# Rows of v 160 bytes apart in SBUF instead of 130, and two q and two k buffers fewer: an attention-and-FFN kernel on one core

## The chip, the cores and the metric

The kernel runs on one core of one Trainium2 chip. The metric is the device time of one execution in microseconds (us). Runs of the two kernels of a comparison alternate on one chip.

In the views, PE is the TensorE, PEld its weight loads, DVE the VectorE, ACT the ScalarE, POOL the GpSimd and SP the SyncE. A run of bytes is a stretch of adjacent bytes that one packet writes. A load has landed when its last completion event has come. k2 is the load of k for block 2, and so on.

## The reference, cut to what matters

```python
# q, k, v: (4, 8, 768, 64) f32; 4 sink positions, window 128
scores = scale * np.matmul(q, k.transpose(0, 1, 3, 2))
keep = is_sink | in_window          # a query sees 4 sinks and the last 128 keys
a = softmax(np.where(keep, scores, -1e9))
x = np.matmul(a, v)                 # -> (3072, 512)
xn = x / rms(x) * rms_g
out = (silu(xn @ w_gate) * (xn @ w_val)) @ w_out    # d_ff 1536
```

The work is cut into 24 blocks of 128 query positions (4 batches of 6). Each block needs its own q, k and v: three loads of 128 rows x 8 heads x 64 numbers.

## The kernel before: the parts that matter

```python
VW = D + 1                          # 65: 64 numbers of v and a 1.0 that sums the weights
LD = 16                             # buffers for q, and as many for k
ld  = ctx.enter_context(tc.tile_pool(name="ld", bufs=LD))
vld = ctx.enter_context(tc.tile_pool(name="vld", bufs=B))
...
V16 = {b: vld.tile([P, NT, H, VW], BF16, name="v16") for b in range(B)}
...
for b in range(B):                  # the column of ones
    dve(60, lambda b=b: nc.vector.memset(V16[b][:, :, :, D:VW], 1.0), ...)
...
def load_v(g):                      # f32 in HBM, cast to bf16 by the load
    b, t = divmod(g, NT)
    nc.gpsimd.dma_start(out=V16[b][:, t, :, 0:D], in_=block_of(v, g))
...
def av(g, u):                       # the matmuls that read v
    ...
    nc.tensor.matmul(
        out=dest, lhsT=T["e", g, u][:, x, 0, :], rhs=V16[b][:, t, h, :],
        start=(t == 0), stop=True, skip_group_check=True,
    )
```

A row of `V16` is one head of one position: 64 bf16 of v, 128 bytes, and then the 1.0. With `VW = 65` rows lie 130 bytes apart, so few start on a multiple of 32. The program decides the order of all instructions at build time with a small model of the engines (`Plan`); `LD` is also a constraint of that model: a load of q or k of block g comes after the transpose of block g - LD.

The softmax here doesn't subtract the row's maximum and nothing guards it: scores larger than these inputs give would overflow.

Of the kernel before, what the change touches and what calls it, by code (L numbers as in the profile page):

```python
# [12 lines left out]
BF16 = mybir.dt.bfloat16  # L13
I32 = mybir.dt.int32

P = 128
# [10 lines left out]
class Plan:  # L27
# [9 lines left out]
    def __init__(self):  # L37
        self.ops, self.held = [], {}
        self.rings = {"POOL": 0, "HW": 0, "TR": 0}
        self.banks = {i: 0 for i in range(8)}  # L40
# [8 lines left out]
    def land(self, ring, first, work):  # L49
# [3 lines left out]
        if ring == "POOL":  # L53
            begin = max(first, r["POOL"], r["HW"])
            r["POOL"] = begin + (1.4 * work if begin < 8500 else work)
            self.loads -= 1
            return r["POOL"] + 520
        if ring == "HW":
            begin = max(first, r["HW"])
            r["HW"] = begin + (1.25 * work if begin > 2500 else work)  # L60
            return r["HW"] + 900
        begin = max(first, r["TR"], r["POOL"])
# [74 lines left out]
def kernel(  # L137
# [15 lines left out]
    B, H, S, D = q.shape  # L153
# [5 lines left out]
    NT = S // P  # L159
# [5 lines left out]
    NG = NB // GB  # L165
    GN = GB * P
    VW = D + 1
    HW = 4 * VW
    SW = P // HP
    inv_sqrt_d = 1.0 / math.sqrt(D)  # L170
# [9 lines left out]
    POOL_MASK_FROM = 16  # L180
    X_DMA_FROM = 9
    QK_DMA_FROM = 8
    LD = 16
    GATE_FROM = 6
    LOAD_LEAD = 9
    LEAD_FROM = 10
# [7 lines left out]
    const = ctx.enter_context(tc.tile_pool(name="const", bufs=1))  # L194
    ld = ctx.enter_context(tc.tile_pool(name="ld", bufs=LD))
    vld = ctx.enter_context(tc.tile_pool(name="vld", bufs=B))
# [16 lines left out]
    def bank(slot):  # L213
        name = "_".join(str(x) for y in slot for x in (y if isinstance(y, tuple) else (y,)))
        BANK[slot] = ring.tile([P, 512], FP32, name=name, tag=f"bank{plan.held[slot]}")
        return BANK[slot]
# [10 lines left out]
    sel = const.tile([P, P], BF16, name="sel")  # L227
    headm = const.tile([P, H], FP32, name="headm")
    grow = const.tile([1, DM], FP32, name="grow")
    V16 = {b: vld.tile([P, NT, H, VW], BF16, name="v16") for b in range(B)}  # L230
    T = {}


# [18 lines left out]
    for b in range(B):  # L252
        dve(60, lambda b=b: nc.vector.memset(V16[b][:, :, :, D:VW], 1.0),
            gives=[("vone", b)], prio=-97 + b if b == 0 else -50)
# [54 lines left out]
    def block_of(src, g):  # L309
        b, t = divmod(g, NT)  # L310
        return src[b, :, t * P:(t + 1) * P, :].rearrange("h t d -> t h d")
# [9 lines left out]
    def load_bf16(name, src, g):  # L321
        T[name, g] = ld.tile([P, H, D], BF16, name=name)
        nc.gpsimd.dma_start(out=T[name, g], in_=block_of(src, g))  # L323

    def load_v(g):
        b, t = divmod(g, NT)
        nc.gpsimd.dma_start(out=V16[b][:, t, :, 0:D], in_=block_of(v, g))  # L327

# [4 lines left out]
    for i, name in enumerate(F32_LOADS):  # L333
        n, g, e = name[0], int(name[2:]), {"s": "SP", "a": "ACT"}[name[1]]
# [7 lines left out]
        out=grow, in_=moe_rms_g.rearrange("(o d) -> o d", o=1)))}, (), ["grow"], -89.5,  # L342
# [5 lines left out]
    def sw_load(fn, gives, work, ns=870, needs=()):  # L348
        n = len(issue)
        more = [("sw", n - DEPTH)] if n >= DEPTH else []  # L350
        op({"POOL": (ns, 1900, fn)}, list(needs) + more, list(gives) + [("sw", n)], -89 + n,
           ring="POOL", work=work)
        issue.append(n)

    def sw_block(g, what="qkv"):
        for n in what:
# [3 lines left out]
            else:  # L360
                src = q if n == "q" else k
                needs += [(n + "T", g - LD)] if g >= LD else []
                sw_load(lambda n=n, src=src, g=g: load_bf16(n, src, g), [(n, g)], 860,
# [137 lines left out]
    def av(g, u):  # L501
        b, t = divmod(g, NT)
        pv = bank(("av", g, u))
        if t >= 2:
            nc.tensor.matmul(  # L505
                out=pv[:, 0:HW], lhsT=T["esk", g], rhs=T["vsk", b][:, 4 * u:4 * u + 4, :],
                start=True, stop=False, skip_group_check=True,
            )
        for j in range(2):
            for hi in range(2):  # L510
                h = 4 * u + 2 * j + hi
                x = 2 * hi + j
                dest = pv[:, (h - 4 * u) * VW:(h - 4 * u + 1) * VW]
                if t >= 1:
                    nc.tensor.matmul(  # L515
                        out=dest, lhsT=T["e", g - 1, u][:, x, 1, :],
                        rhs=V16[b][:, t - 1, h, :],
                        start=(t == 1), stop=False, skip_group_check=True,
                    )
                nc.tensor.matmul(  # L520
                    out=dest, lhsT=T["e", g, u][:, x, 0, :], rhs=V16[b][:, t, h, :],
                    start=(t == 0), stop=True, skip_group_check=True,
                )
        T.pop(("e", g - 1, u), None)

    def normal(g, u):
        if u == 0:
            T["x16", g] = xpool.tile([P, H, D], BF16, name="x16")
        pvv = BANK.pop(("av", g, u))[:, 0:HW].rearrange("p (h c) -> p h c", c=VW)
        rden = small.tile([P, 4], FP32, name="rden")  # L530
# [72 lines left out]
    def sink_v(b, half):  # L603
        nc.tensor.matmul(
            out=bank(("vs", b, half))[:, 0:HW], lhsT=sel,
            rhs=V16[b][:, 0, 4 * half:4 * half + 4, :], start=True, stop=True,
        )

    def sink_vm(b, half):
        if half == 0:  # L610
            T["vsk", b] = sink.tile([P, H, VW], BF16, name="vsk")
        hs = slice(half * 4, half * 4 + 4)
# [34 lines left out]
    for g in range(NB):  # L647
        b, t = divmod(g, NT)
# [40 lines left out]
        for u in range(2):  # L689
            xs = [[("x", g, u, hi, n) for hi in range(2)] for n in range(nq)]  # L690
            if g < PE_MASKS:
                es = xs
            elif g < POOL_MASK_FROM or t == 0:
                dve(600 if nq == 2 else 335, lambda g=g, u=u: mask_dve(g, u),
                    sum(xs, []) + ["masks"], [("e", g, u)], early)
                es = [[("e", g, u)]] * nq
            else:
                es = []
                for n in range(nq):
                    pool(590, lambda g=g, u=u, n=n: mask_pool(g, u, n), sum(xs, []),  # L700
                         [("e", g, u, n)], g)
                    es.append([("e", g, u, n)])
            T["es", g, u] = es
            needs = es[0] + (T["es", g - 1, u][1] if t else []) + [("v", g), ("vone", b)]
            needs += [("v", g - 1)] if t else []
            needs += [("esk", b, t), ("vsk", b, 0), ("vsk", b, 1)] if t >= 2 else []
            needs += [("av", g - 1, u)] if g else []
            pe((130, 242, 354)[min(t, 2)], lambda g=g, u=u: av(g, u), needs, [("av", g, u)],
               pa + 5, takes=[("av", g, u)])
            dve(548, lambda g=g, u=u: normal(g, u),  # L710
                [("av", g, u)] + ([("xr", g - 3)] if g >= 3 else [])
                + ([("n", g - 1, u)] if g else []), [("n", g, u)], early, drops=[("av", g, u)])
# [19 lines left out]
        if t == 0:  # L732
            dve(600, lambda b=b: sink_k(b),
                [("kT", g), ("s", g + 1)] + ([("ss", b - 2, i) for i in ((2, 4) if b - 2 < 2 else (2,))]
                               if b >= 2 else []), [("ksk", b)], 0.1 * g)
            for half in range(2):
                pe(115, lambda b=b, half=half: sink_v(b, half), [("v", g), ("vone", b), "sel", ("s", g)],
                   [("vs", b, half)], pa + 14, takes=[("vs", b, half)])
                dve(340, lambda b=b, half=half: sink_vm(b, half), [("vs", b, half), "headm"]
                    + ([("av", NT * (b - 2) + NT - 1, u) for u in range(2)] if b >= 2 else [])  # L740
                    + ([("vsk", b, 0)] if half else []),
                    [("vsk", b, half)], 0.1 * g, drops=[("vs", b, half)])
            for t0, n in ((2, 2), (4, 2)) if b < 2 else ((2, 4),):
                pe(n * 53 + 16, lambda b=b, t0=t0, n=n: sink_s(b, t0, n),
                   [("ksk", b), ("s", g + 1)] + [("qT", g + t0 + i) for i in range(n)],
                   [("ss", b, t0)], -1000.0 + 10 * (g + t0) + 2, takes=[("ss", b, t0)], mode=3)
                act(n * 107 + 55, lambda b=b, t0=t0, n=n: sink_e(b, t0, n),
                    [("ss", b, t0), "table"] + ([("av", g - 1, u) for u in range(2)] if b else []),
                    [("esk", b, t0 + i) for i in range(n)], early, drops=[("ss", b, t0)])
# [169 lines left out]
```

## Time and profile before

| | |
|---|---|
| time, median of the first 3 runs | 246.64 us (246.4 to 246.71) |
| span of the profiled execution | 244.3 us |
| TensorE (PE) busy | 232.6 us, 95% |
| transfers queued by GpSimd (POOL), share of 16 engines | 81.0% (76.6% in another execution of the same kernel, e2 below) |
| q, k and v loads | 70, 128 KB each in SBUF, median 10.4 to 10.9 us from issue to landing |
| matmuls that read v | 352 of 65 columns, 8 of 260 |

The page of the profile gives busy times, then forty slices of the span, the transfer queues and the chain of work that ended last. A busy engine need not be one that sets the time; the chain and the waits say which one does. The lines themselves stand in the prediction.

### The profile page before, as it was taken

What the parts mean: (1) busy time and instruction counts of PE and PEld (TensorE: products, weight loads), DVE (VectorE), ACT (ScalarE), POOL (GpSimd) and SP (SyncE); (2) the same over time, 40 slices, a digit from 0 to 9 for tenths busy, and PEclk for the clock granted to TensorE, in tenths of its full rate; (3) what the DMA queues carried; (4) which work ended last, traced back from release to release, by engine and by line L of the source; (5) the groups of instructions that cost most, each with busy time, mean ns of one, the idle gap of its engine ahead of it and who ended that gap; (6) DMA issues with size and microseconds to landing.
All of it is one profiled execution on the core that took longest, in us unless ns stands there. A gap on an engine that the chain in (4) does not pass through costs nothing.

```text
span 244.3 us, 5510 instructions
## 1 busy us (share of the span) xinstructions
PE 232.6 (95%) x2098; PEld 147.8 (61%) x2120; DVE 183.7 (75%) x482; ACT 131.2 (54%) x276; POOL 88.8 (36%) x114
## 2 busy tenths in 40 slices
PE   4978999999999999999999999999999999999994
PEld 2557996875789765688875444444545544444443
DVE  4388979979899998899888499991299992377700
ACT  3886466778675837654537555735745521333111
POOL 8995755695444749423004200302504200000000
PEclk9999999999999999999999999999999999999999
DMA  8999999999999999999944544014311013200022
GB/s 112 172 170 195 192 188 188 156 146 174 171 196 130 156 124 179 142 216 133 149 35 107 133 107 86 3 21 108 120 34 21 4 21 107 86 3 0 0 86 86
DMA packets 111979, 27.22 MB, mean 111 GB/s; under 512 B 102097, under 2 KB 109009, under 8 KB 111954
## 3 DMA queue, kind: packets, MB, share of 16 engines
q0 software_dynamic: 80704, 13.90, 81.0%
q1 hardware_dynamic: 31106, 12.85, 27.0%
q8 instruction: 16, 0.26, 0.5%
q10 hardware_dynamic: 144, 0.13, 0.2%
q14 instruction: 9, 0.07, 0.1%
HBM read 28.31 MB, written 6.29 MB: 142 GB/s over the span
## 4 chain that ended last, share of the span: by engine, by line
PE 77%; DVE 9%; POOL 5%; DMA 4%; issue 3%; ACT 0%; POOLq 0%; DVEq 0%; ACTq 0%
PE o L790 23%; PE g L757 21%; PE v L757 21%; PE s L456 4%; DMA wg<-in_moe_w_gate_dram 4%; DVE hT L780 2%; PE av L520 2%; DVE p L770 2%; PE av L515 2%; DVE r L560 2%; POOL v L327 1%; DVE xr L564 1%; PE av L505 1%; PE o_last L808 1%; DVE x L532 1%
## 5 line engine op out<-in xcount | busy, mean ns | idle before, releaser
L757 PE MATMUL g<-xnt,wg 128*128 128x128 bf16 (+2 forms) x525 | 69.8, 282 | 1.6 <-DMA wg<-in_moe_w_gate_dram 1.2
L757 PE MATMUL v<-xnt,wv 128*128 128x128 bf16 (+2 forms) x522 | 71.0, 281 | 0.3
L764 ACT ACTIVATE th<-g 128x512 bf16<-128x512 f32 x72 | 42.9, 600 | 46.7 <-PE g L757 45.2
L790 PE MATMUL o<-wo,hT 128*128 128x512 bf16 x263 | 62.6, 379 | 1.2 <-issue 0.6
L770 DVE SCALAR_TENSOR_TENSOR p<-th,g 128x512 bf16<-128x512 bf16 x72 | 48.1, 683 | 16.6 <-ACT th L764 16.2
L757 PEld LDWEIGHTS <-wg 128*128 128x128 bf16 x528 | 43.1, 98 | 21.0 <-DMA wg<-in_moe_w_gate_dram 1.5
L757 PEld LDWEIGHTS <-wv 128*128 128x128 bf16 x528 | 42.6, 98 | 18.5 <-issue 0.8
L469 ACT ACTIVATE e<-s 128x512 bf16<-128x512 f32 (+1 forms) x104 | 48.4, 542 | 6.6 <-PE s L456 6.3
L780 DVE TENSOR_TENSOR hT<-p,v 128x512 bf16<-128x512 bf16 x72 | 47.2, 682 | 1.5 <-PE v L757 0.6
L790 PEld LDWEIGHTS <-hT 128*128 128x128 bf16 x276 | 25.6, 98 | 28.7 <-issue 1.3
L491 POOL TENSOR_SCALAR_AFFINE_SELECT e<-e 128x512 bf16<-128x512 bf16 x14 | 9.4, 680 | 61.8 <-ACT e L469 48.8
L798 ACT ACTIVATE osb<-o 128x512 f32<-128x512 f32 x23 | 13.8, 599 | 29.0 <-PE o L790 29.0
L323 POOL DMA_DIRECT2D k<-in_k_dram x23 | 20.5, 890 | 15.9 <-DMA v<-in_v_dram 7.0
L323 POOL DMA_DIRECT2D q<-in_q_dram x23 | 20.5, 893 | 13.0 <-DMA k<-in_k_dram 3.8
L327 POOL DMA_DIRECT2D v<-in_v_dram x24 | 21.3, 889 | 10.0 <-DMA q<-in_q_dram 6.0
L532 DVE TENSOR_TENSOR x<-av,rden 128x256 bf16<-128x256 f32 x48 | 20.4, 425 | 1.7
L540 ACT ACTIVATE sq<-x 128x512 bf16<-128x512 bf16 x24 | 15.2, 632 | 9.4 <-DVE x L532 9.3
L531 DVE RECIPROCAL rden<-av 128x4 f32<-128x4 f32 x48 | 8.5, 177 | 15.4 <-PE av L520 15.3
L486 DVE TENSOR_TENSOR e<-e,masks 128x1024 bf16<-128x1024 bf16 (+1 forms) x30 | 18.9, 650 | 1.0 <-ACT e L469 0.8
L564 DVE SCALAR_TENSOR_TENSOR xr<-x,r,gb 128x512 bf16<-128x512 bf16 x24 | 19.0, 790 | 0.9
L520 PE MATMUL av<-v,e 128*128 128x65 bf16 x192 | 16.9, 194 | 0.0
L515 PE MATMUL av<-v,e 128*128 128x65 bf16 x160 | 15.0, 193 | 0.0
(70 smaller groups left out, 177.2 us busy)
## 6 DMA issues: line engine op xcount, KB each, us to landing
out_dram<-osb SPq DMA_DIRECT2D x23, 256.0 KB, 2.2
v<-in_v_dram POOLq DMA_DIRECT2D x24, 128.0 KB, 10.4
q<-in_q_dram POOLq DMA_DIRECT2D x23, 128.0 KB, 10.9
k<-in_k_dram POOLq DMA_DIRECT2D x23, 128.0 KB, 10.8
wo<-in_moe_w_out_dram POOLq DMA_DIRECT2D x2, 768.0 KB, 12.0
wg<-in_moe_w_gate_dram POOLq DMA_DIRECT2D x4, 256.0 KB, 7.8
wv<-in_moe_w_val_dram POOLq DMA_DIRECT2D x4, 256.0 KB, 8.2
wg<-in_moe_w_gate_dram POOLq DMA_DIRECT2D x1, 384.0 KB, 9.4
```

Source lines behind the costliest of these rows:

```text
L323: nc.gpsimd.dma_start(out=T[name, g], in_=block_of(src, g))
L327: nc.gpsimd.dma_start(out=V16[b][:, t, :, 0:D], in_=block_of(v, g))
L469: nc.scalar.activation(out=T["e", g, u][:, 2 * hi:2 * hi + 2, n0:n1, :].rearrange("p x n c -> p x (n c)"), in_=ps.rearrange("p (j c) -> p ...
L515: nc.tensor.matmul(out=dest, lhsT=T["e", g - 1, u][:, x, 1, :], rhs=V16[b][:, t - 1, h, :], start=(t == 1), stop=False, skip_group_check=True,
L520: nc.tensor.matmul(out=dest, lhsT=T["e", g, u][:, x, 0, :], rhs=V16[b][:, t, h, :], start=(t == 0), stop=True, skip_group_check=True,)
L532: nc.vector.tensor_tensor(out=T["x16", g][:, 4 * u:4 * u + 4, :], in0=pvv[:, :, 0:D], in1=rden.unsqueeze(2).to_broadcast((P, 4, D)), op=AL ...
L564: nc.vector.scalar_tensor_tensor(out=T["xr", g], in0=T.pop(("x16", g)).rearrange("p h d -> p (h d)"), scalar=r[:, 3:4], in1=gb, op0=ALU.mu ...
L757: nc.tensor.matmul(out=ps[:, i * n:(i + 1) * n], lhsT=w_sb[:, kt, ft * P:(ft + 1) * P], rhs=T["xnt", G][:, kt, cols], start=(kt == 0), sto ...
L764: nc.scalar.activation(out=T["th", key], in_=BANK[("g", key)], func=ACT.Tanh, scale=0.5,)
L770: nc.vector.scalar_tensor_tensor(out=T["p1", key], in0=T.pop(("th", key)), scalar=1.0, in1=BANK.pop(("g", key)), op0=ALU.add, op1=ALU.mult,)
L780: nc.vector.tensor_tensor(out=T[hk][:, i:i + n, cols], in0=T.pop(("p1", key)).rearrange("p (n c) -> p n c", n=n), in1=BANK.pop(("v", key)) ...
L790: nc.tensor.matmul(out=BANK[("o", G, tb)], lhsT=T["h", G, ft // 4][:, ft % 4, tb * P:(tb + 1) * P], rhs=wo[:, ft, :], start=(ft == 0), sto ...
```

## The change

The intent: every 128-byte run of v that a load writes is to start on a multiple of 32 bytes and fill whole 32-byte pieces, so that no neighbouring bytes have to be kept. That any are kept otherwise was a guess. The price is memory: 4 batches x 48 rows x 30 bytes = 5,760 bytes on each partition. With all 16 q/k buffers that does not fit: the builder then finds 8.625 KB left for the last pool, which needs 10. Two q and two k buffers fewer free 4 KB.

```diff
+    VS = 80
...
-    LD = 16
+    LD = 14
...
-    V16 = {b: vld.tile([P, NT, H, VW], BF16, name="v16") for b in range(B)}
+    V16 = {b: vld.tile([P, NT, H, VS], BF16, name="v16") for b in range(B)}
...
-                        rhs=V16[b][:, t - 1, h, :],
+                        rhs=V16[b][:, t - 1, h, 0:VW],
...
-                    out=dest, lhsT=T["e", g, u][:, x, 0, :], rhs=V16[b][:, t, h, :],
+                    out=dest, lhsT=T["e", g, u][:, x, 0, :], rhs=V16[b][:, t, h, 0:VW],
...
-            rhs=V16[b][:, 0, 4 * half:4 * half + 4, :], start=True, stop=True,
+            rhs=V16[b][:, 0, 4 * half:4 * half + 4, 0:VW], start=True, stop=True,
```

## The prediction

> **What bounds the kernel now.** I read the page from the top: busy shares, the forty slices, the chain that ended last. The first question for a change of layout is whether transfers, the TensorE or something else sets the end.
>
> ```profile
> PE 232.6 (95%) x2098; PEld 147.8 (61%) x2120; DVE 183.7 (75%) x482; ACT 131.2 (54%) x276; POOL 88.8 (36%) x114
> PE   4978999999999999999999999999999999999994
> DMA  8999999999999999999944544014311013200022
> PE 77%; DVE 9%; POOL 5%; DMA 4%; issue 3%; ACT 0%; POOLq 0%; DVEq 0%; ACTq 0%
> ```
>
> The TensorE (PE) is at 9 from the fourth slice (18 us) to the tail and carries 77% of the chain. The transfer engines are at 9 up to slice 20 (122 us), but the chain puts only 4% on transfers. So a transfer sets the pace early only. The chain in order of time shows where:
>
> ```profile
> 14.58 0.62 POOL wv L369
> 15.21 9.42 DMA wg<-in_moe_w_gate_dram
> 24.63 0.05 issue
> 24.68 1.51 PE g L757 x24
> ```
>
> Up to 24.68 us the chain is POOL issuing loads, then one weight load; after that it is PE work. The waits of PE agree: its longest on a transfer is this one, 1.2 us in two waits.
>
> ```profile
> PE g L757 <- DMA wg<-in_moe_w_gate_dram: 1.2, 2, 1.0
> ```
>
> So a faster or slower v load can move the end through the first 25 us; later only if a load became so late that PE ran dry. A changed cost of a matmul that reads v would count everywhere.
>
> **What the Trainium skill says, and whether the trace agrees.** (1) "DMA: Bandwidth & Descriptors", section Specifications: below 512 B a transfer does not reach line rate, because the engine does a read-modify-write. Each run of v that lands in SBUF is 64 bf16 = 128 B, before and after, so by that rule both layouts are on the slow side. The page does not say what the start address adds. (2) The same page, "Why small descriptors are slow (HBM only)": a packet has about 3 cycles of overhead, so 256 B cost 256/32 + 3 = 11 cycles. The f32 source run here is 256 B for q, k and v alike; 11 cycles at the 850 MHz that the page gives are an estimate of 12.9 ns per packet. The trace: one load is 128 rows x 8 heads = 1,024 packets, 64 on each of 16 transfer engines. Counting the software queue's packets in order of their starts, the windows below hold q2, k2, v2, q3, k3, one load each:
>
> ```profile
> 11.18:12.03 0.85, 0.85 (x8) 0.39 (x5) 0.81 (x5) 0.69 (x3) 0.85 (x2) 1.00 2.42 154
> 12.03:12.88 0.85, 0.75 (x12) 0.34 (x10) 0.69 (x4) 0.85 (x4) 0.85 (x2) 1.00 2.44 155
> 12.88:13.73 0.85, 0.74 (x14) 0.69 (x14) 0.71 (x6) 0.82 (x3) 0.85 (x2) 1.00 2.43 155
> 13.73:14.58 0.85, 0.18 (x5) 0.12 (x3) 0.85 (x2) 0.00 (x0) 0.85 (x3) 1.00 2.42 154
> 14.58:15.42 0.84, 0.84 (x21) 0.63 (x20) 0.77 (x5) 0.52 (x2) 0.84 (x3) 1.00 2.42 154
> ```
>
> The last two columns are the transfer engines' share and GB/s. The third row is v2, whose runs lie 130 B apart; the others are q and k with runs 128 B apart, all starting on 32-byte lines. All take 0.84 to 0.85 us, 0.85 us / 64 = 13.3 ns per packet, close to the page's read-side estimate. The misaligned start costs nothing that this view can see. (3) "TensorE: Matmul & The Clock Gate", "Back-to-back issue gap": N/2.4 + 2.5 ns when warm, for the 65 columns of a v row an estimate of 29.6 ns. The timeline of PE, eight matmuls on v between two others:
>
> ```profile
> 21.74 0.27 PE L505 MATMUL av<-vsk,esk 128*128 128x260 bf16 x1
> 21.85 0.19 PE L515 MATMUL av<-v,e 128*128 128x65 bf16 x1
> 21.88 0.19 PE L520 MATMUL av<-v,e 128*128 128x65 bf16 x1
> ...
> 22.06 0.19 PE L520 MATMUL av<-v,e 128*128 128x65 bf16 x1
> ```
>
> The next matmul, of the gate, starts at 22.09, so eight take 0.24 us, 30.0 ns each: at the streaming rate already. (4) "SBUF — State Buffer", section Door 1, the note on cachelines: lines are 16 B, each new line costs. A run of 130 B touches 9 lines if it starts on one, and 9 or 10 otherwise; the 30.0 ns leave no room for a visible penalty, so the trace shows none of it.
>
> **The change, part by part.** The order of instructions on each engine is the same before and after, up to line numbers; I compared the two listings. No instruction is added or removed. Three things move.
>
> *v rows at 160 B instead of 130.* 24 loads write them. v2 cost what k2 and q3 cost, so I put the saving per load at 0 to 0.01 us. Only v0 to v3 lie ahead of the weight load that sets 24.68 us: 4 x 0.01 = 0.04 us at most. The matmuls that read v: 192 + 160 = 352 of 65 columns. At most 30.0 - 29.6 = 0.4 ns each is left to gain, 352 x 0.4 = 0.14 us. Some groups elsewhere in the trace have starts 33 to 35 ns apart in two of eight places; summed over all of them the excess over 29 ns is under 0.7 us, part of it waits for weights or for the exponentials. So 0 to 0.5 us off PE, my central value 0.1. The 8 matmuls that spread the sink rows (260 columns) read four runs instead of one; even 10 ns more each would be 0.08 us, and they lie in the gaps of PE.
>
> *Two q and two k buffers fewer (14 instead of 16).* The q and k loads from block 14 on now wait for readers of an older tile. Block 14's loads wait for readers of block 0, which ran near 7 us; the timeline of POOL has q14 issued at 65.84 us. The latest releaser is a transposing transfer of block 8, for q19:
>
> ```profile
> 47.96 1.29 SPq L430 DMA_TRANSPOSE qkT<-q  x1
> 90.97 0.89 POOL L323 DMA_DIRECT2D q<-in_q_dram  x1
> ```
>
> Issued at 47.96 us, with the slowest landing of such a transposition at 8.6 us in the view of that tile, it is done by 56.6 us, 34 us before q19. All new waits are met when they are reached. The program's own pacing rule, which holds back a load until the scores nine blocks earlier are done, is stricter than a depth of 14. Cost 0; some waits are listed with one or two semaphores more, perhaps 0.02 us of POOL each, where POOL is idle 13.0 to 15.9 us in total before its q and k loads anyway (groups of the page).
>
> *One wait less.* The listing shows that the first load of each batch into v waited for the memset of the column of ones, and no longer does, presumably because with 160 B rows the two share no 32-byte piece. The memsets end by 2.2 us; v0 is issued at 3.82 us, right behind POOL's own mask work. Gain 0.
>
> Sum: 0 (loads) - 0.1 (PE) + 0 (buffers, waits) = -0.1 us. 246.64 - 0.1 is 246.5 us.
>
> **The rivals.** *Aligned writes are cheaper.* This is the intent: with 32-byte pieces whole, nothing is patched. If each v load shrank by a quarter, 0.21 us, v0 to v3 would bring the gate weights 0.85 us sooner and the end would be near 245.8 us (0.3%). Against it: the equal windows; for it: only that the chain of the first 25 us runs through these loads. *Aligned writes are slower by beats.* The skill's first page, "How a descriptor splits into AXI transactions", counts 32-byte beats from the 256-byte line below a start. I estimate, over eight heads, 60 beats at 160 B against 55 at 130 B and 48 at 128 B. Were these what counts, v2 would already take 55/48 of k2, 0.97 us, and it takes 0.85. If starts 224 B into a line (11 beats) fell behind the read side, a load might grow by 10%, four by 0.34 us: near 246.9. *The buffers bite.* If the late loads were delayed by a new wait, POOL idle before q and k loads would grow after 65 us and PE would show waits on transfers there. It would take over 30 us of delay before q19; I give it 1%. *PE reads get cheaper*, by all the excess found: 246.0 us.
>
> **Range and chances.** The largest single effect I can construct is 0.9 us, 0.35%; three runs before spread 0.3 us, and another chip or occasion may shift both by some tenths. The 8-in-10 range is 245.9 to 247.2 us. A change over 2% needs 4.9 us, five times any of these: 1% faster, 1% slower, 98% within 2%.
>
> **What would show it.** Right: windows of v loads still 0.85 us, like k and q; eight v matmuls still in 0.23 to 0.24 us; the gate weights still ending the early wait at 24.5 to 24.8 us; POOL's waits in the second half unchanged. Wrong: a v window that is no longer equal to its neighbours, with the early chain shifted by four times the difference; a matmul on v at another pace; or a wait of PE on q, k or v after 60 us. I would be wrong beyond the range if the shifted addresses of all later tiles changed the pace of engines that I have not looked at, which nothing here suggests.

## The result, and the profile after

| | before | after |
|---|---|---|
| time, median of 6 runs | 246.8 us (246.4 to 247.16) | 246.56 us (246.28 to 247.11) |
| ratio after/before, 95% interval | | 0.9995, 0.9979 to 1.0012 |
| span of the profiled execution | 244.3 us | 244.7 us |

A ratio here and below is the mean time of one kernel's runs over the mean of the other's runs of the same rounds, so it is not quite the ratio of the medians in the table. Executions over 1.5% slower than the fastest of the same kernel are left out of the means. The time did not change: the interval allows a gain of 0.2% and a loss of 0.1%.

The page of the changed kernel, its busy shares, two of the slices' rows and the chain by engine:

```profile
PE 235.8 (96%) x2120; PEld 148.7 (61%) x2120; DVE 183.4 (75%) x482; ACT 131.1 (54%) x276; POOL 88.6 (36%) x114
PE   4898999999999999999999999999999999999994
DMA  7999999999999999999913644014311013200022
PE 82%; DVE 10%; issue 2%; DMA 2%; ACT 2%; SPq 0%; DVEq 0%; ACTq 0%
```

The busy shares are those of before within a point; POOL's 5% and the transfers' 4% of the chain have become 0 and 2%. PE is busy 3.2 us longer than in the first profile of before. Some 0.9 us of that goes with 22 matmul records more (2,120 against 2,098; a trace can lack some). The rest is not of the change: e1 and e2 below, one of each kernel, have 234.9 and 235.0 us with the 2,098 records of before, which had 232.6; they start slowly, and that one did not. The stretches that held q2, k2, v2 and q3, found by counting packets as in the prediction (columns: stretch, length, busy time of PE, PEld, DVE, ACT and POOL with counts, granted clock, share of the transfer engines, GB/s; the share is the summed time of the packets over 16 engines, here over 1):

```profile
11.46:12.31 0.85, 0.85 (x16) 0.65 (x16) 0.00 (x0) 0.80 (x3) 0.85 (x3) 1.00 2.43 155
12.31:13.16 0.85, 0.85 (x11) 0.71 (x9) 0.70 (x4) 0.85 (x4) 0.85 (x3) 1.00 2.42 154
13.16:14.00 0.84, 0.84 (x6) 0.48 (x5) 0.84 (x3) 0.44 (x2) 0.84 (x2) 1.00 2.42 154
14.00:14.85 0.85, 0.85 (x4) 0.25 (x2) 0.66 (x4) 0.34 (x2) 0.85 (x2) 1.00 2.43 155
```

The third is v2: by this view it takes what the others take, as before. The timeline of PE, eight matmuls on v:

```profile
23.21 0.19 PE L516 MATMUL av<-v,e 128*128 128x65 bf16 x1
...
23.42 0.20 PE L521 MATMUL av<-v,e 128*128 128x65 bf16 x1
23.45 0.38 PE L758 MATMUL g<-xnt,wg 128*128 128x128 bf16 x4
```

From 23.21 to 23.45 is 0.24 us for eight, 30 ns each, as before: reading v at another stride saves PE nothing.

Two things did differ. First, the start. The chain in order of time of the changed kernel begins with a load of q and then PE, not with POOL and weights:

```profile
1.84 4.83 DMA stage<-in_q_dram
6.67 0.02 issue
6.70 0.63 ACT q L320
7.32 0.05 issue
7.37 1.03 PE q L417 x8
```

and PE waits for no weights any more; the list of its waits has no transfer in it. Second, a view that I had not read for single loads: the time from issue to landing. Of the loads in flight for the 10 ns from 8.80 us, k2 and v2, before:

```profile
k<-in_k_dram POOLq DMA_DIRECT2D x1, 128.0 KB, 5.9
v<-in_v_dram POOLq DMA_DIRECT2D x1, 128.0 KB, 6.1
```

and after:

```profile
k<-in_k_dram POOLq DMA_DIRECT2D x1, 128.0 KB, 6.1
v<-in_v_dram POOLq DMA_DIRECT2D x1, 128.0 KB, 6.1
```

k2 and v2 are issued 0.87 us apart in both and their packets start 0.85 us apart, but before, v2 took 0.2 us longer to land than k2. (What counts is the difference between k2 and v2 of one execution: from one execution to another the whole queue moves by 0.1 to 0.3 us.) So the misaligned write may cost something, at a place where the packets' starts do not show it. The experiments had to say what these two differences are, and why neither reaches the end.

### The profile page after: what moved, and what is told of

The parts are those of the page before. It is cut to its first block, busy times and chain, and to the rows that moved or that the text cites. A ratio compares the mean times of both kernels' runs of the same rounds, so it can differ in the third digit from the quotient of the medians.

```text
span 244.7 us, 5533 instructions
## 1 busy us (share of the span) xinstructions
PE 235.8 (96%) x2120; PEld 148.7 (61%) x2120; DVE 183.4 (75%) x482; ACT 131.1 (54%) x276; POOL 88.6 (36%) x114
## 4 chain that ended last, share of the span: by engine, by line
PE 82%; DVE 10%; issue 2%; DMA 2%; ACT 2%; SPq 0%; DVEq 0%; ACTq 0%
PE o L791 23%; PE v L758 22%; PE g L758 22%; PE s L457 5%; PE av L521 2%; DVE hT L781 2%; DMA stage<-in_q_dram 2%; DVE p L771 2%; DVE r L561 2%; PE av L516 2%; DVE xr L565 2%; PE av L506 1%; PE o_last L809 1%; DVE x L533 1%; PE x L580 1%
## 5 line engine op out<-in xcount | busy, mean ns | idle before, releaser
L791 PE MATMUL o<-wo,hT 128*128 128x512 bf16 x276 | 64.5, 379 | 0.1
L532 DVE RECIPROCAL rden<-av 128x4 f32<-128x4 f32 x48 | 8.5, 177 | 16.5 <-PE av L521 16.4
L521 PE MATMUL av<-v,e 128*128 128x65 bf16 x192 | 17.3, 196 | 0.3 <-ACT e L470 0.3
L457 PE MATMUL s<-qkT 64*128 64x256 bf16 (+1 forms) x208 | 14.6, 262 | 0.6 <-ACT qkT L424 0.6
```

The source lines that it names most:

```text
L457: nc.tensor.matmul(out=BANK[slot][:, j * 256 + n0 * P:j * 256 + n1 * P], lhsT=qkT[pr, 1, hp, t * P:(t + 1) * P], rhs=qkT[pr, 0, hp, (t + n ...
L521: nc.tensor.matmul(out=dest, lhsT=T["e", g, u][:, x, 0, :], rhs=V16[b][:, t, h, 0:VW], start=(t == 0), stop=True, skip_group_check=True,)
L791: nc.tensor.matmul(out=BANK[("o", G, tb)], lhsT=T["h", G, ft // 4][:, ft % 4, tb * P:(tb + 1) * P], rhs=wo[:, ft, :], start=(ft == 0), sto ...
```

## The experiments

Landing times to 0.01 us below are worked out from the completion events in the trace, which the view above prints in tenths. A load's landing counts when all of its 16 shares have arrived.

### e1: the changed kernel again, and e2: the kernel before against itself

No edit in either. Five rounds each, on one chip.

> The changed kernel once more, to narrow the interval and to get a second profile of its first 25 us. Theory (nothing of the change lies on the path that sets the end): ratio to the kernel before 0.998 to 1.002. Rival (aligned writes bring the first weights sooner, or cheaper reads of v): ratio 0.9965 or less. Of the first 25 us: if the late first gate matmul in the first profile of the changed kernel came from the start of this one execution, the new profile will show the attention matmuls of block 0 about 30 to 36 ns apart in some execution and 54 ns in others; if the change causes it, 54 ns again.

> The kernel before against itself. It shows how far two sets of runs of one and the same program differ: expected ratio 0.998 to 1.002. If its ratio or its first 25 us differ as much as those of the changed kernel did, none of these differences belongs to the change.

Measured: e1 246.91 us, ratio to before 1.0007 (0.9992 to 1.0021). e2 246.81 us, ratio 1.0000 (0.9982 to 1.0018). The changed kernel stands to before as before stands to itself. The rival of a gain of 0.35% is outside e1's interval.

The start: the first eight matmuls of 65 columns begin 32 to 38 ns apart in the first profile of before, and 49 to 57 ns apart in the profiles of after, e1 and e2, and of e3, e4, e8, e10 and e11 as well. These eight in the first profile of before and in e2:

```profile
10.25 0.43 PE L520 MATMUL av<-v,e 128*128 128x65 bf16 x8
11.86 0.62 PE L520 MATMUL av<-v,e 128*128 128x65 bf16 x8
```

The kernel before has a slow start too, in e2; its one fast start was a feature of that execution. With it goes the wait for weights. The waits of PE in e2, all but a wait called issue:

```profile
PE s L438 <- DVE bias L273: 2.1, 1, 2.1
PE warm L391 <- DVE zeros L258: 1.1, 1, 1.1
PE q L416 <- ACT q L319: 0.8, 1, 0.8
...
PE s L456 <- DVE qkT L423: 0.6, 1, 0.6
PE x L579 <- DVE xr L564: 0.4, 1, 0.4
```

No transfer. The Trainium skill, "TensorE: Matmul & The Clock Gate", Part 1, says that the array runs at half its clock until it has been busy for one window of about 3.4 us, and that this window runs freely, so that executions differ. 65 columns at the page's 1.2 GHz are 54.2 ns, and the trace has 53 to 57 for most; this agrees. The granted clock that the profile prints was 1.00 in these stretches all the same. So the first difference between the two profiles is not of the change.

The landings, as time from the landing of k2 to that of v2, and so on:

| | rows of v | k2 to v2 | v2 to q3 | k3 to v3 | v3 to weights | fourth gate weights land at |
|---|---|---|---|---|---|---|
| before | 130 B | 1.04 | 0.82 | 0.97 | 2.17 | 24.63 |
| e2 | 130 B | 1.05 | 0.80 | 0.94 | 0.76 | 24.31 |
| e3 (below) | 130 B | 1.04 | 0.80 | 0.94 | 0.76 | 24.48 |
| after | 160 B | 0.82 | 0.96 | 0.58 | 1.24 | 24.47 |
| e1 | 160 B | 0.84 | 0.96 | 0.56 | 1.25 | 24.71 |
| e4 (below) | 160 B | 0.83 | 0.96 | 0.60 | 1.21 | 24.88 |

(The weights after v3 are the second of six loads of gate weights; the fourth is the one that PE waited for in the first profile of before.) With rows 130 bytes apart v2 lands some 0.21 us later and v3 some 0.4 us later than with 160, in all six profiles. It is so for v4, v5, v6 and v8 too: 0.98 to 1.09 us after their k in the three profiles at 130 bytes, 0.82 to 0.89 us in the three at 160. The next load then follows sooner, and the weights after v3 land at the same time: 18.38 us in e2 and in e1. In the first profile of before they landed at 19.71 us (the 2.17 in its row), against 18.38 to 18.58 in the five others; that is one execution, and e2 and e3 with the same layout don't show it. The landings lag behind the packets' starts and catch up: no wait of PE on v is listed in any of the six, and the fourth gate weights land at 24.31 to 24.63 us with rows 130 bytes apart, 24.47 to 24.88 with 160, not earlier.

### e3: the buffers alone

```diff
-    LD = 16
+    LD = 14        # rows of v left 130 bytes apart
```

> 14 instead of 16 q and k buffers, rows of v left 130 bytes apart. Theory: all new waits are met before they are reached, ratio 0.998 to 1.002, POOL waits for nothing new between 60 and 116 us. Rival (two effects of the change cancel: a gain from the rows, a loss from the buffers): ratio over 1.003 here.

Measured: 246.93 us, ratio 1.0002 (0.9989 to 1.0015). Of POOL's waits, those of q and k loads on older tiles would be on the transposes of q and k, by transfer or by PE: the list has none. (The q and k loads wait 1.9 us in all for matmuls of scores, PE s, which do not read those tiles; the program's own pacing rule makes loads wait for scores.) The waits of the q and k loads at the head of the list are those on loads eight places earlier, the depth of the queue in the program:

```profile
POOL k L323 <- DMA v<-in_v_dram: 11.4, 7, 2.8
...
POOL q L323 <- DMA k<-in_k_dram: 4.0, 3, 2.2
```

Before had 7.0 and 3.8 us there, the changed kernel 7.9 and 5.4: they vary with the loads' landings and cost PE nothing. No cancelling pair of effects.

### e4: ten buffers

```diff
-    LD = 14
+    LD = 10        # on the changed kernel; the order of instructions stays
```

> The changed kernel with 10 q and k buffers instead of 14, same order of instructions. Theory: the reused tile was read at least 20 us before the load that takes it, still no wait; ratio 0.998 to 1.002. Rival (a depth of 14 already costs a little): 10 costs more, ratio over 1.003 and waits of POOL on transposing transfers or on PE transposes.

Measured: 246.5 us, ratio 0.9986 (0.9974 to 0.9999). Not a gain to claim: it is 0.14%, e2, one program against itself, has a wider interval, and nothing that I found in the profile would make it. POOL's list has no wait on transposes (one of 0.6 us is put down to ACT qkT, a copy of transposed q or k that reads none of these buffers). For the theory it is enough that ten buffers are no slower.

### e5: loads alone, software queue

Only loads, with the stride of the written rows as the one difference, ten loads of 4,096 runs each; the output is zeros. The loop, shortened:

```python
for what, stride in (("tight", 65), ("wide", 80), ("dense", 64)):
    for n in range(10):
        t = pool.tile([P, 32, stride], BF16, name=name)      # int16 for "plain"
        nc.gpsimd.dma_start(out=t[:, :, 0:64], in_=src)      # "cast": 256 B of f32
                                                             # "plain": 128 B as they are
```

> Loads alone, wrong output on purpose. Ten loads of 4096 runs of 128 bytes each into rows 130 bytes apart (tight), then 160 (wide), then 128 (dense), first cast from 256-byte f32 source runs as the kernel does, then plain copies of 128-byte source runs. Theory (the read of 256 bytes sets the pace of a packet, so the write is hidden): cast at 3.39 us a load for all three strides; plain loads are quicker[...]. There tight may then cost more than wide, by 10% or more, if a misaligned write costs anything at all. Rival (a misaligned write is free in itself): plain tight equals plain wide within 2%. Rival (aligned writes cheaper in the cast too): cast tight over cast wide by 3% or more.

Measured, as the distance between two issues in POOL's timeline once the queue is full. Columns: start, length, instruction, idle time before it.

```profile
25.83 1.68 POOL L54 DMA_DIRECT2D cast_tight<-in_v_dram  x1 [2.39 <-issue]
29.89 1.67 POOL L54 DMA_DIRECT2D cast_tight<-in_v_dram  x1 [2.38 <-issue]
...
59.30 1.67 POOL L54 DMA_DIRECT2D cast_wide<-in_v_dram  x1 [1.64 <-issue]
62.60 1.67 POOL L54 DMA_DIRECT2D cast_wide<-in_v_dram  x1 [1.62 <-issue]
...
90.03 1.67 POOL L54 DMA_DIRECT2D cast_dense<-in_v_dram  x1 [1.94 <-issue]
93.64 1.67 POOL L54 DMA_DIRECT2D cast_dense<-in_v_dram  x1 [1.93 <-issue]
```

Cast: tight 4.06, wide 3.30, dense 3.61 us a load. Plain: tight 4.07, wide 3.31, dense 2.41 us. My theory had 3.39 for all casts: it fell. The rival that aligned writes are cheaper in the cast too, by 3% or more, was right: tight over wide is 1.23. The difference of tight and wide is the same whether 256 or 128 bytes are read, so the writing side makes it. Per run it is 0.76 us x 16 engines / 4,096 = 3.0 ns, and for one load of the kernel, 64 runs on each engine, 0.19 us. That is close to the 0.21 us by which v2 landed later. The dense rows are not settled: 3.61 us here as a cast, 2.41 plain, and 3.33 in e9 below, where their buffers lie at other addresses; whether that is the reason was not tested. I rest nothing on them.

### e6: the same from SyncE's queue

> The three strides as plain copies of 128-byte source runs from SyncE's queue. Theory as for the plain loads of the software queue: tight over wide by 10% or more if a misaligned write costs anything once the read no longer hides it; the rival says equal within 2%.

The tile view of the three groups; the numbers are the least, median and greatest time that SyncE spent on one, which is held up by the queue:

```profile
L54 SPq DMA_DIRECT2D plain_tight<-in_v_dram x10: 434/4008/4148, 0.7 to 32.8; - x10
...
L54 SPq DMA_DIRECT2D plain_wide<-in_v_dram x10: 3178/3251/4012, 37.0 to 67.8; - x10
...
L54 SPq DMA_DIRECT2D plain_dense<-in_v_dram x10: 3226/3538/3633, 71.1 to 103.1; - x10
```

Tight over wide is 23% again, so neither the cast nor the software queue is the cause.

### e7: loads alone, in the kernel's own shape

The same with loads of 1,024 runs, once from the kernel's own source addresses, once from near ones.

> Loads alone again, wrong output on purpose, because the run before showed 4.08 us for 4096 runs written 130 bytes apart against 3.31 us at 160, while the kernel's own v loads show no difference. Now loads of 1024 runs, ten for each stride (130, 160, 128, 130 again), first from the kernel's own source addresses (eight heads, far apart in HBM), then from runs that lie near one another as in the run before. POOL issues one load in about 0.87 us, so anything quicker hides. Theory A (in the kernel's shape, 8 runs a row, the misaligned write stays hidden, and it needs 32 runs in a row or near sources to show): kern tight at 0.87 us as kern wide. Theory B (the kernel hid it by luck or by its other traffic): kern tight at 1.02 us a load or more, 64 x 15.9 ns. If near tight is at 1.02 us and kern tight at 0.87, the source addresses decide; if both are at 0.87, the number of runs in a row decides.

The timeline of POOL, where a row joins loads that follow one another without idle time:

```profile
1.27 5.43 POOL L57 DMA_DIRECT2D kern_tight<-in_v_dram  x6 [0.82 <-PEq L90]
6.90 0.88 POOL L57 DMA_DIRECT2D kern_tight<-in_v_dram  x1 [0.19 <-issue]
7.96 0.87 POOL L57 DMA_DIRECT2D kern_tight<-in_v_dram  x1 [0.18 <-issue]
9.01 1.84 POOL L57 DMA_DIRECT2D kern_tight<-in_v_dram  x2 [0.18 <-issue]
10.84 4.38 POOL L57 DMA_DIRECT2D kern_wide<-in_v_dram  x5
```

Six tight loads go out at 0.9 us each, then the issues stand 1.05 us apart, the tight rate (64 x 15.9 ns = 1.02). The packets of the third to seventh load start at 13.5 to 14.8 ns a run on each engine, those of the ninth and tenth at 16.5 and 15.9. So theory B holds once the queue is full of tight loads; for the first few the lag is taken up and not seen in the packets' starts. The starts of the later phases are disturbed by waits for buffers, and I don't read kern against near from them. The landings tell them apart all the same: kern tight loads land 0.96 to 1.06 us apart from the third on, and near tight loads 0.97 to 0.99 us apart in the first five, while kern wide and near wide loads land 0.81 to 0.92 and 0.77 to 0.89 us apart from the first to the fifth. So neither the source addresses nor the number of runs in a row decides. The kernel has one tight load in three, which fits its staying in the part where the lag is taken up.

### e8: q and k off the 32-byte lines too

```diff
+    QO = 2           # elements: 4 bytes
+    def rows_of(name, g):
+        o = QO if 0 < g < QK_DMA_FROM else 0
+        flat = ld.tile([P, H * D + 16], BF16, name=name)
+        return flat[:, o:o + H * D].rearrange("p (h d) -> p h d", d=D)
...
-        T[name, g] = ld.tile([P, H, D], BF16, name=name)
+        T[name, g] = rows_of(name, g)
```

(on the kernel before, with 14 buffers; the second change at both places where a tile is made)

> The kernel before with more misaligned writes: besides v, the q and k loads of blocks 1 to 7 now start 4 bytes off a 32-byte line (14 buffers to make room, same order of work). The landings of the earlier runs showed v landing 0.2 us later when its rows are 130 bytes apart, and the following loads and weights unchanged. Theory (the write side falls behind by about 0.2 us a misaligned load and makes it up in the next weight load, PE does not need it earlier): q, k and v of blocks 2 and 3 land up to 1 us later, the first weights after them at most 1 us later, and the time stays within 0.998 to 1.003. Rival (the loads of the first 25 us set the end): every delay of the weights appears at the end, ratio 1.003 or more.

Measured: 246.78 us, ratio 0.999 (0.9968 to 1.0011). The time is as expected, the landings are not. q1, the first load of the queue and itself shifted, lands 0.23 us later than in e2 (7.01 against 6.78 us; 6.62 to 6.94 in the other profiles without a shift), whether by the shift or by the execution is not told. After that nothing is added: the first weights land at 10.02 against 9.77 us, and q2, k2, q3 and k3 are 0.18 to 0.25 us later than in e2; k2 to v2 is 0.98, k3 to v3 0.93 us. So starting 4 bytes off a 32-byte line is not by itself what made v late by 0.2 to 0.4 us. It need not be free: e9 below has 3.61 against 3.33 us for this shift, which would be 0.07 us for one load of the kernel, too little to see here.

### e9: which alignment it is

Loads alone as in e5, eight of each layout, 4,096 runs of 128 bytes each.

```python
for name, stride, first in (        # elements of 2 bytes: row to row, ahead of the first row
    ("by_tight", 65, 0), ("by_four_bytes", 66, 0), ("by_eight_bytes", 68, 0),
    ("by_sixteen_bytes", 72, 0), ("by_wide", 80, 0), ("dense_off_two", 64, 1),
    ("dense_off_four", 64, 2), ("dense", 64, 0),
):
```

> Loads alone, wrong output on purpose: eight cast loads of 4096 runs of 128 bytes for each of eight layouts: rows 130, 132, 136, 144 and 160 bytes apart, then rows 128 bytes apart that start 2, 4 and 0 bytes off a line. Known: 130 takes 4.07 us a load, 160 takes 3.33, 128 takes 3.61. Open is what makes 130 slow, since q and k loads starting 4 bytes off a line cost nothing in the kernel. Theory L (a 32-byte line written in part costs): all but 160 and the aligned 128 take about 4.07. Theory F (a run that does not start on 4 bytes costs): only 130 and the 2-byte shift take 4.07, 132, 136 and 144 about 3.3 to 3.6. Theory H (a gap that leaves a line with a hole costs): 130, 132, 136, 144 take about 4.07, both shifted dense layouts 3.61.

The view of the transfers, median us from issue to landing with the queue full:

```profile
by_tight<-in_v_dram POOLq DMA_DIRECT2D x8, 512.0 KB, 11.9
by_four_bytes<-in_v_dram POOLq DMA_DIRECT2D x8, 512.0 KB, 10.5
...
by_wide<-in_v_dram POOLq DMA_DIRECT2D x8, 512.0 KB, 9.6
dense_off_two<-in_v_dram POOLq DMA_DIRECT2D x8, 512.0 KB, 17.5
dense_off_four<-in_v_dram POOLq DMA_DIRECT2D x8, 512.0 KB, 10.5
```

| rows written | starts off 4 bytes | us a load, from the packets' starts |
|---|---|---|
| 130 B apart | every other one | 4.07 |
| 132 B apart | none | 3.60 |
| 136 B apart | none | 3.54 |
| 144 B apart | none | 3.46 |
| 160 B apart | none | 3.33 |
| 128 B apart, shifted 2 B | all | 5.94 |
| 128 B apart, shifted 4 B | none | 3.61 |
| 128 B apart | none | 3.33 in most (two at 3.50 and 3.38) |

Theory F: what costs is a run that does not start on a multiple of 4 bytes. Half of them so gives 4.07, all of them 5.94, none 3.33 to 3.61. My number for the 2-byte shift (4.07 as well) was too low. Of the 0.74 us from 130 to 160 bytes, 0.47 is won by 132 already; the other 0.27 comes with the wider rows, and the alignment and the gap between rows grow together there, so the runs don't say which of them it is. Nor is the cost in proportion to the runs that start off: half of them add 0.47 us (to 132-byte rows), all of them 2.33 us (to the 4-byte shift). In 128-byte rows shifted by 2 bytes two neighbouring runs also share a 4-byte word, which I did not separate from the start.

### e10: rows 132 bytes apart, all 16 buffers

```diff
+    VS = 66
...
-    V16 = {b: vld.tile([P, NT, H, VW], BF16, name="v16") for b in range(B)}
+    V16 = {b: vld.tile([P, NT, H, VS], BF16, name="v16") for b in range(B)}
```

(and `0:VW` at the three reads, as in the change)

> Rows of v 132 bytes apart instead of 130 and all 16 q and k buffers kept, so the rows alone change. The loads by themselves took 3.6 us at 132 against 4.07 at 130. Theory F (only a start off 4 bytes costs, and the kernel doesn't need v sooner): v0 to v3 land close to the loads before them, as with 160-byte rows (v2 0.80 to 0.90 us after k2, not 1.04), time unchanged, ratio 0.998 to 1.002. Rival (the two missing buffers hid a gain of the aligned rows): ratio 0.997 or less.

Measured: 246.8 us, ratio 0.9999 (0.9982 to 1.0016). k3 to v3 is 0.77 us, between 0.94 (130 B) and 0.56 to 0.60 (160 B); k2 to v2 is 0.98, where I expected 0.80 to 0.90: a miss, the gain is about a third of that of 160-byte rows at v2 (0.06 of 0.21 us) and half at v3. v4 and v5 land 0.84 and 0.88 us after their k, as with 160, v6 and v8 0.97 and 0.98. So in the kernel the start off 4 bytes explains a part of the lag that varies from load to load; the rest is open. The time: no gain was hidden by the buffers. This was the nearest thing to a better version, since it keeps the buffers, and it isn't faster.

### e11: a large dose

```diff
-    QO = 2
+    QO = 1           # e8 with q and k of blocks 1 to 7 shifted 2 bytes
```

> The kernel before with 14 buffers, and q and k of blocks 1 to 7 starting 2 bytes off, the layout that took 5.94 us by itself where 4 bytes off took 3.61. A large dose of late landings in the first 25 us. Theory: the write side now falls behind by about 0.6 us for each of the six q and k loads ahead of the weights, more than the weight loads can make up: the gate weights that land near 24.5 us land 2 to 4 us later, PE shows waits on transfers there, and the time grows by 1.5 to 4 us, ratio 1.006 to 1.016. Rival (landings of the first 25 us never reach the end): ratio 0.998 to 1.003.

Measured: 251.97 us, ratio 1.0194 (1.0172 to 1.0216): slower by 4.8 us (0.0194 x 246.9), past my 4 us. The fourth gate weights land at 27.06 instead of 24.31 us (e2), k6 at 50.85 instead of 46.03, k7 at 57.42 instead of 51.45. PE now waits on transfers:

```profile
PE k L422 <- DMA k<-in_k_dram: 1.6, 4, 1.0
PE q L422 <- ACT q L325: 1.2, 1, 1.2
PE warm L397 <- DVE zeros L259: 1.1, 1, 1.1
PE q L422 <- DMA q<-in_q_dram: 0.9, 2, 0.5
```

The largest of them comes at 50.89 us, before the transposes of k6:

```profile
50.89 0.40 PE L422 MATMUL k<-ident,k 128*128 128x128 bf16 x4 [0.99 <-DMA k<-in_k_dram]
```

The six waits on transfers are 2.4 us together, at 8.9, 19.9, 35.5, 42.4, 50.9 and 57.5 us, each for a q or k load. None is for the gate weights, where I had expected them: landing 2.75 us late, these still cost no wait of PE. The profiled execution is the quickest of the five (250.63 us), and its span of 248.9 us is 3.9 us over that of e2. Of these, PE is idle for 2.6 (12.6 against 10.0 us), nearly all of it these waits, and busy for 1.3 (236.3 against 235.0 us, 2,098 records in both). A part of the busy time is slower matmuls: the second group of eight on v starts 73 and then 54 to 56 ns apart, in e2 72, 54, 48, 36 and then 29. Reading the shifted tiles is no rival: the transposing matmuls on q and k take 255 and 243 ns in the mean, against 254 and 243 in e2. The four other executions, up to 1.7 us slower, have no profile. What the run settles: late landings of loads that PE needs do reach the end when they are large, here 3 to 6 us at q4 to k7. So the 0.2 to 0.4 us of the tight rows were harmless because they were small and caught up, not because landings never count.

## Why the prediction was right, and where its working was wrong

The range (245.9 to 247.2), the centre (246.5 against 246.56) and the class held. That the centre came so close is luck: the gain of 0.1 us behind it is smaller than the spread of either kernel's runs (0.8 us), and the kernel before measured 246.64 and 246.8 us. Step by step:

1. *The TensorE sets the time.* Right: 82% of the chain after and in e2, 77% in the first profile of before.
2. *A load of v saves 0 to 0.01 us.* Wrong by a factor of twenty. The step read the equal windows of packets and took them for the transfer's cost. A packet's record shows when it was started; the time at which a load has landed showed 0.21 us for v2, and loads alone put 0.19 us on each. The rival "aligned writes are cheaper" had guessed 0.21 us a load and was right in that size for v2. It was wrong in the next step, that four such savings would bring the gate weights 0.85 us sooner: v3's 0.4 us were made up by the weights behind it, which landed at 18.38 us in e1 and e2 alike. So the result was right in part by luck, for a reason I did not have: the cost exists and is caught up.
3. *By the skill's estimate of 11 cycles, 256 bytes of f32 hide the write.* Not borne out as I used it. I called it a read-side estimate, but the page ("DMA: Bandwidth & Descriptors", "Why small descriptors are slow") speaks of the bus between the reading and the writing half. Plain loads of 128-byte sources took the same 4.07 and 3.31 us at 130 and 160 bytes.
4. *The rival "slower by beats".* Fell: no layout in e9 is quicker than 160-byte rows, though they cost the most beats.
5. *PE reads of v gain 0.1 us.* Within its own 0 to 0.5: eight matmuls in 0.24 us before and after, nothing to see. One count of the prediction is off: 65 numbers of 2 bytes touch 9 lines of 16 bytes from every even start, never 10, so by that note the two layouts cost PE the same.
6. *The buffers cost nothing.* Right, e3 and e4. Two readings of the listing were off, without effect: POOL has one semaphore instruction more after the change (165 instructions against 164), and q23 waits for a transposition later than block 8's, issued at 52.74 us in the profile of before, 57 us ahead of it.
7. *The gate weights end the early wait at 24.5 to 24.8 us.* Half wrong. They landed at 24.47 us, but the wait was not there in after, e1 or e2. The chain that I read for the first 25 us belonged to one execution in which PE had started at full rate; the chain of another execution of the same kernel (e2) runs through a load of q, PE, VectorE and ScalarE there. One profile was too few for a statement on a start-up phase.

## What to carry to other kernels

Read a load's cost from its landing, against that of the load before it in the same queue, not from the starts of its packets; then ask whether anything waits for that landing before the lag is made up. Rows of bf16 with one added element (65, 130 bytes) put every other write 2 bytes off a multiple of 4; one more element of padding removed 0.47 of 0.74 us of that cost in loads alone, at 2 bytes a row instead of 30, and a third to all of the lag in this kernel. In a kernel that the TensorE sets, and where each such load is followed by others that let the writes catch up, it buys no time. In loads alone, one after another, rows 160 bytes apart took 3.30 us where rows 130 apart took 4.06; a kernel whose pace such loads set was not tried.

## What the Trainium skill lacked or had wrong

- "DMA: Bandwidth & Descriptors" says nothing of destinations that do not start on 4 bytes. Here 4,096 runs of 128 bytes took 5.94 us when all started 2 bytes off, 4.07 when every other one did, 3.33 to 3.61 when none did.
- The same page, Specifications: below 512 B a transfer does a read-modify-write and misses line rate. The runs do not show what is a read-modify-write; they show that among 128-byte runs the time differs by a factor of 1.8 (5.94 over 3.33 us) by where they start, which the entry doesn't let one expect.
- The same page, "How a descriptor splits into AXI transactions": counted for the written rows, its beats order 128, 130, 160 bytes from cheap to dear. Measured in one run: 128 and 160 at 3.33 us, 130 at 4.07. The section speaks of bytes fetched and has nothing on written rows; these runs do not follow it there.
- The same page, "Why small descriptors are slow (HBM only)": 11 cycles for 256 bytes, an estimate of 12.9 ns at 850 MHz; 160-byte rows took 13.0 ns a run (3.33 us x 16 / 4,096). But plain loads of 128-byte sources took the same 3.31 us at 160, so the agreement does not show that reading sets the pace.
- The same page, "Two DMAs through the same engine are not ordered", has an engine's reads and writes in separate queues, but gives no size for the lag of a load's landing behind its packets' starts and does not say that following loads make it up: v3 landed 0.4 us later with rows 130 bytes apart, the weights behind it at the same 18.38 us.
- "TensorE: Matmul & The Clock Gate", Part 1, agrees with the starts 53 to 57 ns apart for 65 columns in a slow start; but the profile's granted clock printed 1.00 there, so the half rate has to be read from the distance of the starts.
